# Scores and values' products of the first two batches as whole float32 products, with the order planned anew

## The chip, the cores and the metric

The kernel runs on one core of one Trainium2 chip. A core has five engines that run side by side and wait for each other by semaphores: TensorE (PE; its weight loads, PEld, stand as an engine of their own), VectorE (DVE), ScalarE (ACT), GpSimd (POOL) and SyncE (SP), which here only issues DMA transfers. The metric is the device time of one execution in microseconds (us), the median of several runs.

## The reference

Three stages follow each other, all in float32, with B=4 batches, 448 positions, 12 heads of 64:

```
scores = q @ k.T / 8 (causal mask); attn = softmax(scores); x = attn @ v      # per batch and head
u  = x + (relu(x.T @ w_tok1) @ w_tok2).T                                     # token mixing
y  = u + relu(u @ w_ch1) @ w_ch2                                             # channel mixing, 768 -> 1536 -> 768
h  = relu(y @ w_in); a, b = halves of h; n = layer norm of b
out = (a * (w_spatial @ n + b_spatial)) @ w_out                              # gated unit
```

q, k, v and w_spatial arrive as float32; the weights of token mixing, channel mixing and w_in, w_out arrive as 64-bit floats and are turned into float32 on the core.

## The kernel before

**Split operands.** Every product of two float32 operands is made of three: each operand is kept as two float32r parts, hi (ACT's cast) and lo (the difference, on POOL or DVE), and PE sums hi·hi, hi·lo and lo·hi (`mm3`, lines 227 to 229, and line 395). The product lo·lo is left out.

**Attention.** It runs over 24 pairs of heads (6 a batch). For pair n, `load` brings q, k (`stage`, first 896 columns) and v (512 columns). `split_qkv` makes `qh`, `ql` from q and k (ACT L343, POOL through L218) and hi and lo of v side by side in `vhl` (POOL, L215 and L218). `scores` issues 24 products (four chunks of queries, three terms, two heads; the heads lie on the two halves of the 64+64 rows), DVE adds the mask and takes the maximum (L403), ACT takes the exponential (L420), POOL normalizes (L437). `transposed` turns the weights over in five groups of 3 or 4 blocks (L478); of each group ACT takes hi (L481) and DVE lo (L218). `weighted` makes 8 products per head (L499 to L505) against `vhl`, so that the 128 output rows hold v's hi part and its lo part; ACT copies one half (L512) and DVE adds the other (L513).

**Token and channel mixing.** After every third pair a half batch goes through `token_mix`. `channel` takes a batch through 24 units: 12 of `ch1` (18 products 448 wide, L227 to L229, `ps<-uhl,whl`) and 12 of `ch2` (two tiles of 9, `ps<-hid,whl`, added to U on DVE, L676). The weights of a unit (`whl`, four buffers that take turns) are converted once: 72 pieces, each with three steps on DVE (L242, L244, L246), one on ACT and one on POOL, through the buffers `conv1`, `conv2` and `conv3`. Units 0 to 3 and 10 to 23 are converted into their `whl` buffer and stored to memory as well, units 4 to 9 come back by a load. `conv2` and `conv3` share their space with U of batches 2 and 3: so the values of pair 12, the first of batch 2, can only be written once the last piece that goes through `conv2` is done.

**The gated unit** comes last. Its weights (`wgv`, 22 pieces, `wf`) are converted into space that attention has left.

**What sets the order.** The kernel first records jobs (engine, planner's cost, keys read and written, priority, earliest start). `Plan.order` places them one by one, and each engine's instructions are issued in that order. Attention goes ahead of channel mixing by priority; pairs below `EAGER` may start at once, later ones at `START + (n - EAGER) * STEP` of the planner's own time.

Of the kernel before, what the change touches and what calls it, by code (L numbers as in the profile page):

```python
# [34 lines left out]

DIRECT = (*range(4), *range(10, 24))

EAGER, START, STEP = 12, 120.0, 28.0


class Buf:
# [128 lines left out]

@with_exitstack
def mixer_kernel(ctx: ExitStack, tc: tile.TileContext, qkv, wtok, wch, wgv, wsp, bsp, out):

# [16 lines left out]
    def buf(tag, shape, dtype, name):  # L192
        return plan.buf(tag, lambda t: sb.tile([128, *shape], dtype, tag=t, name=name))
# [10 lines left out]
    def act(n, psum=True):  # L204
        return (n * 0.833 + (55 if psum else 95)) / 1e3

    def dve(n, psum=True):
        return (n * 1.05 + 60) / 1e3 if psum else (n * 1.09 + 40) / 1e3

    def pool(n, two=True):  # L210
        return (n * 2.35 + 60) / 1e3 if two else (n * 0.83 + 230) / 1e3


    def hi_pool(hi, x):
        nc.gpsimd.tensor_scalar(hi, x, 1.0, 1.0, op0=ALU.mult, op1=ALU.mult)  # L215

    def lo_part(e, lo, x, hi):
        e.tensor_tensor(lo, x, hi.bitcast(F32), op=ALU.subtract)  # L218
# [104 lines left out]
    def load(n):  # L323
        st = stage[n % 2]
        operands[n] = {"st": st}
        p = n - 2.0
        src = qkv[n // NP, n % NP]
        job("SP", 0.07, lambda: nc.sync.dma_start(st.t[:, : 2 * S], src[:, : 2 * S]), w=[(st, "qk")], prio=p, size=458752)
        job("SP", 0.07, lambda: nc.sync.dma_start(st.t[:, 2 * S :], src[:, 2 * S :]), w=[(st, "v")], prio=p + 0.1, size=262144)

    def nominal(n):
        return 0.0 if n < EAGER else START + (n - EAGER) * STEP

    def split_qkv(n):
        st = operands[n]["st"]
        h = buf(f"qh{n % 2}", [2 * S], F32R, "qh")
        l = buf(f"ql{n % 2}", [2 * S], F32R, "ql")
        v = buf(f"v{n % 2}", [8, 128], F32R, "vhl")
        operands[n].update(h=h, l=l, v=v)
        p, at = n - 1.0, max(0.0, nominal(n) - 12)  # L340
        halves = [slice(0, S), slice(S, 2 * S)] if n == 0 else [slice(0, 2 * S)]
        for c in halves:
            job("ACT", act(c.stop - c.start, False), lambda c=c: nc.scalar.copy(h.t[:, c], st.t[:, c]), r=[(st, "qk")], w=[(h, c.start)], prio=p, at=at)  # L343
        for c in halves:
            if n == 0:
                job("DVE", dve(S, False), lambda c=c: lo_part(nc.vector, l.t[:, c], st.t[:, c], h.t[:, c]), r=[(st, "qk"), (h, c.start)], w=[(l, c.start)], prio=p)
            else:
                job("POOL", pool(2 * S), lambda c=c: lo_part(nc.gpsimd, l.t[:, c], st.t[:, c], h.t[:, c]), r=[(st, "qk"), (h, c.start)], w=[(l, c.start)], prio=p, at=at)

        def vs():  # L350
            return st.t[:, 2 * S :].rearrange("p (c d) -> p c d", d=64)

        job("POOL", pool(512, False), lambda: hi_pool(v.t[:, :, 0:64], vs()), r=[(st, "v")], w=[(v, "h")], prio=p + 0.6, at=at)
        job("POOL", pool(512), lambda: lo_part(nc.gpsimd, v.t[:, :, 64:128], vs(), v.t[:, :, 0:64]), r=[(st, "v"), (v, "h")], w=[(v, "l")], prio=p + 0.6, at=at)


    PLACE = {3: (0, 0), 0: (0, S), 2: (1, 0), 1: (1, 320)}
# [1 line left out]
    def scores(n):  # L359

        o = operands[n]
        h, l = o["h"], o["l"]
        big = buf(f"P{n % 2}", [1536], F32, "P32")
        o["big"] = big
        banks = [[bank([2 * j + k], "pss") for k in range(2)] for j in range(2)]
        s = stats[n % 2]
        split_keys = [(x, c) for x in (h, l) for c in ((0, S) if n == 0 else (0,))]

        def P(i):
            if i == 3:  # L370
                return big.t[:, : 2 * S].rearrange("p (j w) -> p j w", j=2)
            if i == 2:
                return big.t[:, 2 * S :].rearrange("p (j w) -> p j w", j=2)
            t = small[n % 2].t
            return (t[:, 0:384] if i == 1 else t[:, 384:512]).rearrange("p (j w) -> p j w", j=2)

        def pk(i, j):
            return (big, i, j) if i > 1 else (small[n % 2], i, j)

        o["P"], o["pk"] = P, pk  # L380

        def ps(i, j):
            k, o_ = PLACE[i]
            M, W = CHUNKS[i][1] - CHUNKS[i][0], CHUNKS[i][1]
            return banks[j][k].t[:M, o_ : o_ + W]

        def mms():
            for i in (3, 2, 1, 0):
                q0, q1 = CHUNKS[i]
                W = q1  # L390
                ks = [slice(2 * S - W, 2 * S), slice(S, S + W)]
                for k, (a, c) in enumerate(((h, h), (h, l), (l, h))):
                    for j in range(2):
                        r = slice(64 * j, 64 * j + 64)
                        nc.tensor.matmul(ps(i, j), a.t[r, q0:q1], c.t[r, ks[j]], start=(k == 0), stop=(k == 2))  # L395

        pkeys = [(banks[j][k], 0) for j in range(2) for k in range(2)]
        job("PE", 1.95, mms, r=split_keys, w=pkeys, touch=[big], prio=n, at=nominal(n))
        for i in (3, 2, 1, 0):
            M, W = CHUNKS[i][1] - CHUNKS[i][0], CHUNKS[i][1]  # L400
            for j in range(2):
                def ttr(i=i, j=j, M=M, W=W):
                    nc.vector.tensor_tensor_reduce(  # L403
                        out=P(i)[:M, j, :],
                        in0=ps(i, j),
                        in1=mask[:M, S - 128 : S - 128 + W] if j == 0 or M == 64 else mask[:M, S - W : S],
                        scale=-1.0 / 8.0,
                        scalar=3.0e38,
                        op0=ALU.add,
                        op1=ALU.min,  # L410
                        accum_out=s.t[:M, 0, 2 * i + j : 2 * i + j + 1],
                    )
# [12 lines left out]
        both = [(s, "sum", i, j) for i in range(4) for j in range(2)]

        def rcp():
            nc.vector.tensor_scalar_add(s.t[:, 2, :], s.t[:, 1, :], 1e-9)
            nc.vector.reciprocal(s.t[:, 2, :], s.t[:, 2, :])  # L429

        job("DVE", 0.15, rcp, r=both, w=[(s, "rs")], prio=n)
        for i in (3, 2, 1, 0):
            M, W = CHUNKS[i][1] - CHUNKS[i][0], CHUNKS[i][1]
            for j in range(2):
                def norm(i=i, j=j, M=M):
                    c = 2 * i + j
# [51 lines left out]
    def weighted(n, j):  # L488
# [22 lines left out]

        job("ACT", 0.55, lambda: nc.scalar.copy(x(), ps.t[64 - 64 * j : 128 - 64 * j, :S]), r=[(ps, 0)], w=[(u, hp, j)], prio=n)  # L512
        job("DVE", dve(S), lambda: nc.vector.tensor_tensor(x(), ps.t[r, :S], x(), op=ALU.add), r=[(ps, 0), (u, hp, j)], w=[(u, hp, j)], prio=n)  # L513


    wt = [buf(f"t{i}", [1536], F32R, f"wt{i}") for i in range(3)]
# [170 lines left out]
                ch2(b, u[1], u[2], i)  # L687


    for n in range(2):  # L690
        load(n)
    split_qkv(0)
    tok_keys = load_tok()
    for i in range(24):
        convert_channel(i)
    for b in range(B):
        U[b] = buf(f"U{b}", [KM, S], F32, f"U{b}")
    for n in range(NPAIR):
        if n:
            split_qkv(n)  # L700
        if n + 2 < NPAIR:
            load(n + 2)
        scores(n)
        for w, j in (("0", 0), ("a", 0), ("b", 0)):
            transposed(n, w, j)
        weighted(n, 0)
        for w in "ab":
            transposed(n, w, 1)
        weighted(n, 1)
        if n % 3 == 2:  # L710
            for s in ("x0", "x1", "x2", "x3", "h0", "h1", "u0", "u1", "u2"):
                token_mix(n // 3, s)
# [327 lines left out]
```

## Time and profile before

| | |
|---|---|
| median of 3 runs | 877.94 us (875.63 to 878.38) |
| profiled execution | 879.76 us, its span 878.0 us |
| granted TensorE clock, mean | 0.975 |
| PE busy | 817.4 us (93%), 4492 products |
| DVE, ACT, POOL busy | 502.9 us (57%), 358.3 us (41%), 345.2 us (39%) |
| DMA | 135.28 MB, mean 154 GB/s |

The busy shares are averages over unlike stretches, so they are read by stretch. Until about 272 us attention, the conversions and the first batch's channel mixing share all engines; until about 475 us PE works on the rest of attention and on channel mixing; then it goes on with channel mixing and the gated unit alone. PE's products overlap, so its busy time is larger than what they cost in a row: the distance between two starts is the price.

### The profile page before, as it was taken

The numbers are of one execution on the slowest core, as the hardware profiler recorded it, in microseconds if no ns is written. First come the engines' busy times: TensorE is split into PE (matmuls) and PEld (weight loads), VectorE is DVE, ScalarE is ACT, GpSimd is POOL, SyncE is SP. The second block draws the span as 40 slices with busy tenths as digits, with TensorE's granted clock in tenths as the row PEclk, the third lists the DMA queues.
The fourth block names the chain that finished last, engine by engine and source line by source line (L and its number), as shares of the span: only waits on it lengthen the run. The fifth ranks groups of instructions, "written<-read, shape, count | busy, mean of one in ns | idle before, by whom it ended". The sixth has DMA issues, their size and how long they took to land.

```text
span 878.0 us, 12877 instructions
## 1 busy us (share of the span) xinstructions
PE 817.4 (93%) x4492; PEld 730.0 (83%) x4492; DVE 502.9 (57%) x1300; ACT 358.3 (41%) x941; POOL 345.2 (39%) x465
## 2 busy tenths in 40 slices
PE   4678889999877999999999998999999999998998
PEld 4567778888766899999999887999998888877997
DVE  6989758898887575656465775312230242275441
ACT  6787857654235565444434223010032232232110
POOL 7978865747563453333334434100051340222000
PEclk9888889999989999999999999999999999999999
DMA  6545514897895243434268798566630000001112
GB/s 233 172 150 186 187 34 121 270 349 251 287 330 209 66 130 136 153 119 165 89 205 266 245 335 271 193 213 216 215 109 1 1 1 1 1 1 50 56 53 94
DMA packets 44273, 135.28 MB, mean 154 GB/s; under 512 B 4656, under 2 KB 12976, under 8 KB 44208
## 3 DMA queue, kind: packets, MB, share of 16 engines
q1 hardware_dynamic: 44208, 134.47, 45.5%
q8 instruction: 35, 0.57, 0.3%
q14 instruction: 30, 0.25, 0.1%
HBM read 110.07 MB, written 24.38 MB: 153 GB/s over the span
## 4 chain that ended last, share of the span: by engine, by line
PE 66%; DVE 19%; DMA 5%; ACT 4%; issue 3%; POOL 2%; SPq 0%; DVEq 0%; POOLq 0%; ACTq 0%
PE ps L227 9%; PE ps L229 9%; PE ps L228 9%; DMA dbl<-in_wgv 4%; PE pss L395 4%; PE pst L478 3%; DVE psw L242 3%; DVE psw L244 3%; DVE P L403 3%; PE pso L227 2%; PE psg L228 2%; PE psg L227 2%; PE psg L229 2%; PE pso L229 2%; PE pso L228 2%
## 5 line engine op out<-in xcount | busy, mean ns | idle before, releaser
L437 POOL TENSOR_SCALAR P<-P,stats 128x448 f32<-128x448 f32 (+1 forms) x192 | 87.4, 477 | 98.7 <-DVE stats L429 91.4
L227 PE MATMUL ps<-hid,whl 128*128 128x448 f32 x288 | 110.1, 382 | 12.1 <-DVE U L676 6.5
L227 PE MATMUL ps<-uhl,whl 128*128 128x448 f32 x288 | 109.5, 380 | 1.1 <-DVE hid L221 0.6
L218 POOL TENSOR_TENSOR uhl<-U,uhl 128x448 fp32r<-128x448 f32 x48 | 54.4, 1162 | 141.9 <-ACT uhl L643 116.8
L229 PE MATMUL ps<-hid,whl 128*128 128x448 f32 x288 | 107.7, 374 | 0.1
L228 PE MATMUL ps<-hid,whl 128*128 128x448 f32 x288 | 107.3, 372 | 0.0
L420 ACT ACTIVATE P<-P,stats 128x448 f32<-128x448 f32 (+1 forms) x192 | 96.1, 505 | 24.4 <-DVE stats L403 24.1
L229 PE MATMUL ps<-uhl,whl 128*128 128x448 f32 x288 | 105.5, 366 | 0.0
L228 PE MATMUL ps<-uhl,whl 128*128 128x448 f32 x288 | 105.4, 366 | 0.0
L676 DVE TENSOR_TENSOR U<-ps,U 128x448 f32<-128x448 f32 x96 | 59.6, 621 | 58.8 <-PE ps L229 58.5
L478 PE MATMUL pst<-ident,P 128*128 128x128 f32 x384 | 63.7, 294 | 21.6 <-POOL P L437 6.8
L403 DVE CUSTOM_DVE_ANT_0 P<-pss,mask 128x448 f32<-128x448 f32 (+1 forms) x192 | 70.2, 417 | 14.5 <-PE pss L395 11.7
L478 PEld LDWEIGHTS pst<-ident,P 128*128 128x128 f32 x384 | 46.4, 149 | 33.9 <-POOL P L437 10.3
L227 PEld LDWEIGHTS ps<-hid,whl 128*128 128x128 f32 x288 | 55.3, 192 | 20.9 <-ACT whl L294 8.2
L221 DVE SCALAR_TENSOR_TENSOR hid<-ps,hid 128x448 fp32r<-128x448 f32 x48 | 29.8, 622 | 57.3 <-ACT hid L660 57.3
L660 ACT ACTIVATE hid<-ps 128x448 fp32r<-128x448 f32 x48 | 26.0, 542 | 86.1 <-PE ps L229 85.8
L229 PEld LDWEIGHTS ps<-hid,whl 128*128 128x128 f32 x288 | 55.3, 192 | 5.8 <-POOL whl L218 0.8
L227 PEld LDWEIGHTS ps<-uhl,whl 128*128 128x128 f32 x288 | 54.2, 188 | 6.4 <-DVE hid L221 0.9
L228 PEld LDWEIGHTS ps<-hid,whl 128*128 128x128 f32 x288 | 55.3, 192 | 4.5
L218 DVE TENSOR_TENSOR Tab<-pst,Tab 128x384 fp32r<-128x384 f32 x96 | 51.3, 550 | 12.7 <-ACT Tab L481 12.3
L229 PEld LDWEIGHTS ps<-uhl,whl 128*128 128x128 f32 x288 | 54.1, 188 | 4.8 <-POOL whl L218 0.2
L481 ACT CAST Tab<-pst 128x384 fp32r<-128x384 f32 x96 | 44.7, 479 | 32.4 <-PE pst L478 31.0
(155 smaller groups left out, 1914.5 us busy)
## 6 DMA issues: line engine op xcount, KB each, us to landing
whl<-unit SPq DMA_DIRECT2D x78, 768.0 KB, 4.3
conv<-in_wch SPq DMA_DIRECT2D x72, 256.0 KB, 3.4
unit<-whl SPq DMA_DIRECT2D x18, 768.0 KB, 4.6
stage<-in_qkv SPq DMA_DIRECT2D x24, 448.0 KB, 3.5
stage<-in_qkv SPq DMA_DIRECT2D x24, 256.0 KB, 3.6
dbl<-in_wgv SPq DMA_DIRECT2D x16, 384.0 KB, 4.0
out_t<-gate SPq DMA_DIRECT2D x24, 224.0 KB, 1.9
unit<-conv SPq DMA_DIRECT2D x18, 256.0 KB, 3.8
```

What stands on the lines that cost most here:

```text
L218: e.tensor_tensor(lo, x, hi.bitcast(F32), op=ALU.subtract)
L221: nc.vector.scalar_tensor_tensor(lo, x, 0.0, hi.bitcast(F32), op0=ALU.max, op1=ALU.subtract)
L227: nc.tensor.matmul(ps, ah, bh, start=(first and i == 0), stop=False)
L228: nc.tensor.matmul(ps, ah, bl, start=False, stop=False)
L229: nc.tensor.matmul(ps, al, bh, start=False, stop=(last and i == n - 1))
L395: nc.tensor.matmul(ps(i, j), a.t[r, q0:q1], c.t[r, ks[j]], start=(k == 0), stop=(k == 2))
L403: nc.vector.tensor_tensor_reduce(out=P(i)[:M, j, :], in0=ps(i, j), in1=mask[:M, S - 128 : S - 128 + W] if j == 0 or M == 64 else mask[:M, ...
L420: nc.scalar.activation(P(i)[:M, j, :], P(i)[:M, j, :], AF.Exp, bias=s.t[:M, 0, c : c + 1], scale=-1.0, accum_out=s.t[:M, 1, c : c + 1])
L437: nc.gpsimd.tensor_scalar(P(i)[:M, j, :], P(i)[:M, j, :], s.t[:M, 2, c : c + 1], 1.0, op0=ALU.mult, op1=ALU.mult)
L478: nc.tensor.transpose(ps.t[:, c : c + M], src, ident[:M, :M])
L481: job("ACT", act(N), lambda: nc.scalar.copy(hl(0), ps.t[:, :N]), r=[(ps, 0)], w=[(b, part)], prio=n)
L676: job("DVE", dve(S), lambda d=d, ps=ps: nc.vector.tensor_tensor(u.t[:, d, :], ps.t[:, :S], u.t[:, d, :], op=ALU.add), r=[(ps, 0), *u_keys( ...
```

## The change

For batches 0 and 1 (pairs 0 to 11) the scores are issued as float32 products of q and k as they arrived (8 for a pair, not 24), with no split. The values are float32 products too: v is loaded into a tile of its own and not split; the transposes go in four groups of four blocks, each left by one copy (two on ACT, two on DVE); one product covers the first 128 columns for both heads, and six more write head 0 to output rows 0 to 63 and head 1 to rows 64 to 127, so that one ACT copy takes both heads to U. Pairs 12 to 23 keep their way. The planner has `EAGER, START, STEP` of 10, 100, 25 in place of 12, 120, 28, and its order is made anew.

```
-EAGER, START, STEP = 12, 120.0, 28.0
+WHOLE_S, WHOLE_V = (0, 1), (0, 1)
+EAGER, START, STEP = 10, 100.0, 25.0
...
+        if n // NP in WHOLE_V:
+            v = buf(f"v{n % 2}", [8, D], F32, "v")
+            operands[n]["v"] = v
+            job("SP", 0.07, lambda: nc.sync.dma_start(v.t, src[:, 2 * S :].rearrange("p (c d) -> p c d", d=D)), w=[(v, "h")], prio=p + 0.1, size=262144)
...
+        whole = n // NP in WHOLE_S
+        if whole:
+            st = o["st"]
+            split_keys, terms = [(st, "qk")], ((st, st),)
+        else:
+            h, l = o["h"], o["l"]
+            split_keys, terms = [(h, 0), (l, 0)], ((h, h), (h, l), (l, h))
+        last = len(terms) - 1
...
-                for k, (a, c) in enumerate(((h, h), (h, l), (l, h))):
+                for k, (a, c) in enumerate(terms):
...
+    def transposed_whole(n):
...
+        for g in range(4):
...
+            if g in (0, 2):
+                job("DVE", dve(N), lambda g=g, ps=ps, N=N: nc.vector.tensor_copy(t.t[:, 512 * g - 512 : 512 * g] if g else t0.t, ps.t[:, :N]), r=[(ps, 0)], w=[(b, g)], prio=n)
+            else:
+                job("ACT", act(N), lambda g=g, ps=ps, N=N: nc.scalar.copy(t.t[:, 512 * g - 512 : 512 * g], ps.t[:, :N]), r=[(ps, 0)], w=[(b, g)], prio=n)
...
+    def weighted_whole(n):
...
+            nc.tensor.matmul(ps.t[:, :S], v.t[:, 0:2, :].rearrange("p c d -> p (c d)"), t0.t, start=True, stop=False, skip_group_check=True)
+            for c, o, w in ((0, 64, 384), (1, 192, 256), (2, 320, 128)):
+                for j in range(2):
+                    r = slice(64 * j, 64 * j + 64)
+                    m = 768 * j + (0, 384, 640)[c]
+                    nc.tensor.matmul(ps.t[r, o:S], v.t[:, 2 + 3 * j + c, :], t.t[:, m : m + w], start=False, stop=(c == 2), skip_group_check=True)
...
+        job("ACT", act(S), lambda: nc.scalar.copy(u.t[:, hp, :], ps.t[:, :S]), r=[(ps, 0)], w=u_keys(n // NP, hp), prio=n)
```

On PE before, the end of the scores of pair 2 and both heads' values of pair 0 (`pss` scores, `pso` values, `T`, `Tab` the turned weights' hi and lo):

```order
L395 MATMUL pss<-qh 64x64 x2
L395 MATMUL pss<-ql,qh 64x64 x2
L395 MATMUL pss<-qh,ql 64x64 x2
L499 MATMUL pso<-T_298,vhl 128x448 x2
L501 MATMUL pso<-Tab,vhl 128x384 x2
L503 MATMUL pso<-Tab,vhl 128x256 x2
L505 MATMUL pso<-Tab,vhl 128x128 x2
L499 MATMUL pso<-T_298,vhl 128x448 x2
L501 MATMUL pso<-Tab,vhl 128x384 x2
L503 MATMUL pso<-Tab,vhl 128x256 x2
L505 MATMUL pso<-Tab,vhl 128x128 x2
```

Now, at the same place, the whole scores of pair 2 and the values of pair 0:

```order
L408 MATMUL pss<-stage_107 128x448 x2
L408 MATMUL pss<-stage_107 128x320 x2
L408 MATMUL pss<-stage_107 128x192 x2
L408 MATMUL pss<-stage_107 64x64 x2
L572 MATMUL pso<-T_254,v 128x448
L577 MATMUL pso<-PT,v 64x384 x2
L577 MATMUL pso<-PT,v 64x256 x2
L577 MATMUL pso<-PT,v 64x128 x2
```

The 24 products of a pair's scores have become 8, and the 16 of its values 7, with 64 output rows in six of them.

On DVE before, the end of the conversions (the steps from `conv` to `psw` and back to `conv`; `U<-pso` is pair 12's values, `U<-ps` channel mixing):

```order
L676 TENSOR_TENSOR U_378<-ps_3181,U_378 128x448
L242 TENSOR_SCALAR psw<-conv_117 128x256
L513 TENSOR_TENSOR U_3209<-pso,U_3209 64x448 x2
L676 TENSOR_TENSOR U_378<-ps_3198,U_378 128x448
L244 SCALAR_TENSOR_TENSOR psw<-conv_117,psw 128x256
L246 SCALAR_TENSOR_TENSOR conv_117<-conv_117,psw 128x256
L218 TENSOR_TENSOR T_3236<-pst,T_3236 128x448
L218 TENSOR_TENSOR Tab<-pst,Tab 128x384 x4
L403 ISA P_3309,stats_66<-pss,mask 128x448
```

Now, at the end of the conversions on DVE:

```order
L743 TENSOR_TENSOR U_312<-ps_2677,U_312 128x448
L245 TENSOR_SCALAR psw<-conv_119 128x256
L247 SCALAR_TENSOR_TENSOR psw<-conv_119,psw 128x256
L249 SCALAR_TENSOR_TENSOR conv_119<-conv_119,psw 128x256
L526 TENSOR_TENSOR U_2721<-pso,U_2721 64x448 x2
L743 TENSOR_TENSOR U_312<-ps_2710,U_312 128x448
L221 TENSOR_TENSOR T_2738<-pst,T_2738 128x448
L221 TENSOR_TENSOR Tab<-pst,Tab 128x384
L743 TENSOR_TENSOR U_312<-ps_2740,U_312 128x448
```

The place is nearly the same: pair 12's values follow the last piece or lie beside it, the scores of pairs 0 to 14 stand ahead of it in both orders, and those of pair 15 behind it. Behind the last `conv` row stand 607 rows of DVE before and 609 now.

## Rows read from the trace of the kernel before

**Rows 1.** Stretches: us, busy us (count) PE PEld DVE ACT POOL, clock, DMA, GB/s.

```profile
0.00:100.00 100.00, 73.51 (x498) 63.00 (x499) 84.58 (x276) 76.65 (x222) 83.05 (x124) 0.88 0.60 193
125.00:200.00 75.00, 73.29 (x470) 65.30 (x470) 65.01 (x189) 48.03 (x134) 44.05 (x62) 1.00 0.66 222
195.00:272.00 77.00, 67.01 (x327) 57.51 (x327) 66.00 (x164) 28.32 (x77) 44.15 (x61) 0.96 0.84 284
0.00:272.00 272.00, 228.05 (x1367) 197.38 (x1368) 225.31 (x665) 167.18 (x471) 184.76 (x266) 0.92 0.65 216
272.00:475.00 203.00, 198.45 (x1253) 182.47 (x1253) 118.67 (x322) 102.26 (x279) 80.38 (x112) 1.00 0.43 143
```

**Rows 2.** Waits from 195 to 272 us: total us, times, longest.

```profile
ACT whl L294 <- DVE conv L246: 46.0, 36, 2.2
```

**Rows 3.** DVE timeline, the last conversion step: start us, us, engine, line, operation.

```profile
271.09 0.42 DVE L246 SCALAR_TENSOR_TENSOR conv<-conv,psw 128x256 uint32<-128x256 uint32 x1
```

**Rows 4.** DVE groups, 0 to 272 us: count, busy us, mean ns, idle.

```profile
L218 DVE TENSOR_TENSOR Tab<-pst,Tab 128x384 fp32r<-128x384 f32 x52 | 27.7, 550 | 3.2 <-ACT Tab L481 2.9
...
L513 DVE TENSOR_TENSOR U<-pso,U 64x448 f32<-64x448 f32 x26 | 16.1, 620 | 3.3 <-ACT U L512 3.0
...
L676 DVE TENSOR_TENSOR U<-ps,U 128x448 f32<-128x448 f32 x22 | 13.6, 617 | 1.1 <-PE ps L229 1.0
...
L218 DVE TENSOR_TENSOR T<-pst,T 128x448 fp32r<-128x448 f32 x13 | 8.1, 620 | 1.7 <-ACT T L481 1.5
L221 DVE SCALAR_TENSOR_TENSOR hid<-ps,hid 128x448 fp32r<-128x448 f32 x12 | 7.4, 620 | 4.2 <-ACT hid L660 4.2
```

**Rows 5.** DVE copy from PSUM (L943): count, ns min/median/max, first and last start.

```profile
L943 DVE COPY gate<-pso x12: 623/624/625, 803.0 to 874.3; 128x448 f32<-128x448 f32 x12
```

**Rows 6.** ACT groups from 0 to 272 us.

```profile
L481 ACT CAST Tab<-pst 128x384 fp32r<-128x384 f32 x52 | 24.2, 478 | 4.7 <-PE pst L478 3.7
...
L343 ACT CAST qh<-stage 128x896 fp32r<-128x896 f32 x16 | 15.1, 941 | 8.9 <-POOL P L437 3.3 <-PE pss L395 2.2 <-DMA stage<-in_qkv 2.1
L512 ACT COPY U<-pso 64x448 f32<-64x448 f32 x26 | 13.7, 527 | 4.9 <-PE pso L505 3.2 <-POOL whl L218 0.8 <-issue 0.2
...
L481 ACT CAST T<-pst 128x448 fp32r<-128x448 f32 x14 | 7.4, 530 | 1.7 <-PE pst L478 1.6
```

**Rows 7.** POOL groups from 0 to 272 us.

```profile
L218 POOL TENSOR_TENSOR ql<-stage,qh 128x896 fp32r<-128x896 f32 x16 | 33.7, 2104 | 6.1 <-ACT qh L343 5.9
L218 POOL TENSOR_TENSOR vhl<-stage,vhl 128x512 fp32r<-128x512 f32 x15 | 19.5, 1299 | 1.2
...
L215 POOL TENSOR_SCALAR vhl<-stage 128x512 fp32r<-128x512 f32 x15 | 9.5, 631 | 7.5 <-PE pso L505 4.9 <-DMA stage<-in_qkv 2.6
```

**Rows 8.** PE timeline around one pair's scores and one head's values.

```profile
396.20 0.36 PE L228 MATMUL ps<-hid,whl 128*128 128x448 f32 x1
396.40 0.37 PE L229 MATMUL ps<-hid,whl 128*128 128x448 f32 x1
396.69 0.47 PE L395 MATMUL pss<-qh 64*128 64x448 f32 x2
397.01 0.37 PE L395 MATMUL pss<-ql,qh 64*128 64x448 f32 x2
...
398.41 0.67 PE L499 MATMUL pso<-T,vhl 128*128 128x448 f32 x2
...
399.67 0.41 PE L227 MATMUL ps<-hid,whl 128*128 128x448 f32 x1
```

**Rows 9.** Chain of waits, a run of seven float32 transposes.

```profile
350.99 0.77 PE pst L478 x7
```

**Rows 10.** The gated unit's conversions, and its first products.

```profile
L246 DVE SCALAR_TENSOR_TENSOR wf<-dbl,psw x22: 501/553/689, 460.6 to 555.3; 128x384 uint32<-128x384 uint32 x16, 128x512 uint32<-128x512 uint32 x6
...
L227 PE MATMUL psg<-uhl,whl x96: 361/365/370, 658.7 to 757.6; 128*128 128x448 f32 x96
```

**Rows 11.** The page's DMA issues: count, KB each, us to landing.

```profile
stage<-in_qkv SPq DMA_DIRECT2D x24, 448.0 KB, 3.5
```

More of the change, by code (lines that the diff above doesn't have):

```diff
@@ L328, in load, with split_qk @@
         job("SP", 0.07, lambda: nc.sync.dma_start(st.t[:, : 2 * S], src[:, : 2 * S]), w=[(st, "qk")], prio=p, size=458752)
-        job("SP", 0.07, lambda: nc.sync.dma_start(st.t[:, 2 * S :], src[:, 2 * S :]), w=[(st, "v")], prio=p + 0.1, size=262144)
+        if n // NP in WHOLE_V:
[3 more added lines that the diff above has]
+        else:
+            job("SP", 0.07, lambda: nc.sync.dma_start(st.t[:, 2 * S :], src[:, 2 * S :]), w=[(st, "v")], prio=p + 0.1, size=262144)
     def nominal(n):
         return 0.0 if n < EAGER else START + (n - EAGER) * STEP
-    def split_qkv(n):
+    def split_qk(n):
         st = operands[n]["st"]
@@ L337, in split_qkv, with split_v @@
         l = buf(f"ql{n % 2}", [2 * S], F32R, "ql")
-        v = buf(f"v{n % 2}", [8, 128], F32R, "vhl")
[L339 to L348, printed above, removed]
+        operands[n].update(h=h, l=l)
+        p, at = n - 1.0, max(0.0, nominal(n) - 12)
+        job("ACT", act(2 * S, False), lambda: nc.scalar.copy(h.t, st.t[:, : 2 * S]), r=[(st, "qk")], w=[(h, 0)], prio=p, at=at)
+        job("POOL", pool(2 * S), lambda: lo_part(nc.gpsimd, l.t, st.t[:, : 2 * S], h.t), r=[(st, "qk"), (h, 0)], w=[(l, 0)], prio=p, at=at)
+    def split_v(n):
+        st = operands[n]["st"]
+        v = buf(f"v{n % 2}", [8, 128], F32R, "vhl")
+        operands[n]["v"] = v
+        p, at = n - 0.4, max(0.0, nominal(n) - 12)
         def vs():
-            return st.t[:, 2 * S :].rearrange("p (c d) -> p c d", d=64)
-        job("POOL", pool(512, False), lambda: hi_pool(v.t[:, :, 0:64], vs()), r=[(st, "v")], w=[(v, "h")], prio=p + 0.6, at=at)
-        job("POOL", pool(512), lambda: lo_part(nc.gpsimd, v.t[:, :, 64:128], vs(), v.t[:, :, 0:64]), r=[(st, "v"), (v, "h")], w=[(v, "l")], prio=p + 0.6, at=at)
+            return st.t[:, 2 * S :].rearrange("p (c d) -> p c d", d=D)
+        job("POOL", pool(512, False), lambda: hi_pool(v.t[:, :, 0:64], vs()), r=[(st, "v")], w=[(v, "h")], prio=p, at=at)
+        job("POOL", pool(512), lambda: lo_part(nc.gpsimd, v.t[:, :, 64:128], vs(), v.t[:, :, 0:64]), r=[(st, "v"), (v, "h")], w=[(v, "l")], prio=p, at=at)
     PLACE = {3: (0, 0), 0: (0, S), 2: (1, 0), 1: (1, 320)}
@@ L361, in scores @@
         o = operands[n]
-        h, l = o["h"], o["l"]
+        whole = n // NP in WHOLE_S
[6 more added lines that the diff above has]
+        last = len(terms) - 1
         big = buf(f"P{n % 2}", [1536], F32, "P32")
@@ L366, in scores @@
         s = stats[n % 2]
-        split_keys = [(x, c) for x in (h, l) for c in ((0, S) if n == 0 else (0,))]
         def P(i):
@@ L391, in mms @@
                 ks = [slice(2 * S - W, 2 * S), slice(S, S + W)]
-                for k, (a, c) in enumerate(((h, h), (h, l), (l, h))):
+                for k, (a, c) in enumerate(terms):
                     for j in range(2):
                         r = slice(64 * j, 64 * j + 64)
-                        nc.tensor.matmul(ps(i, j), a.t[r, q0:q1], c.t[r, ks[j]], start=(k == 0), stop=(k == 2))
+                        nc.tensor.matmul(ps(i, j), a.t[r, q0:q1], c.t[r, ks[j]], start=(k == 0), stop=(k == last))
         pkeys = [(banks[j][k], 0) for j in range(2) for k in range(2)]
-        job("PE", 1.95, mms, r=split_keys, w=pkeys, touch=[big], prio=n, at=nominal(n))
+        job("PE", 2.5 if whole else 1.95, mms, r=split_keys, w=pkeys, touch=[big], prio=n, at=nominal(n))
         for i in (3, 2, 1, 0):
@@ L513, in weighted, with P, block, mms @@
         job("DVE", dve(S), lambda: nc.vector.tensor_tensor(x(), ps.t[r, :S], x(), op=ALU.add), r=[(ps, 0), (u, hp, j)], w=[(u, hp, j)], prio=n)
+    def transposed_whole(n):
+        o = operands[n]
+        def P(i):
+            return o["P"](i).rearrange("p j w -> p (j w)")
+        def block(j, i, c):
+            W, (k0, k1) = CHUNKS[i][1], CHUNKS[c]
+            return P(i)[:, slice(W + k0, W + k1) if j else slice(W - k1, W - k0)]
+        later = [(j, i, c) for j in range(2) for c, i in ((1, 1), (1, 2), (1, 3), (2, 2), (2, 3), (3, 3))]
+        t0 = buf(f"T0{n % 2}", [S], F32, "T0")
+        t = buf(f"A{n % 2}", [12 * 128], F32, "PT")
+        for g in range(4):
+            ps = bank(early if n < NP else banks_tm, "pst")
+            b = t if g else t0
+            N = 512 if g else S
+            keys = [o["pk"](i, j) for i in range(4) for j in range(2)] if g == 0 else [o["pk"](i, j) for j, i, c in later[4 * g - 4 : 4 * g]]
+            def mms(g=g, ps=ps):
+                if g == 0:
+                    blocks = [(q0, P(i)[:, q1 - 64 : q1 + 64]) for i, (q0, q1) in enumerate(CHUNKS)]
+                else:
+                    blocks = [(128 * k, block(*x)) for k, x in enumerate(later[4 * g - 4 : 4 * g])]
+                for c, src in blocks:
+                    nc.tensor.transpose(ps.t[:, c : c + 128], src, ident)
+            job("PE", 0.44, mms, r=keys, w=[(ps, 0)], touch=[b], prio=n)
+            if g in (0, 2):
+                job("DVE", dve(N), lambda g=g, ps=ps, N=N: nc.vector.tensor_copy(t.t[:, 512 * g - 512 : 512 * g] if g else t0.t, ps.t[:, :N]), r=[(ps, 0)], w=[(b, g)], prio=n)
+            else:
+                job("ACT", act(N), lambda g=g, ps=ps, N=N: nc.scalar.copy(t.t[:, 512 * g - 512 : 512 * g], ps.t[:, :N]), r=[(ps, 0)], w=[(b, g)], prio=n)
+        PT[n] = t0, t
@@ new lines, in weighted_whole, with mms @@
+    def weighted_whole(n):
+        v = operands[n]["v"]
+        ps = bank(early if n < NP else banks_tm, "pso")
+        t0, t = PT[n]
+        u = U[n // NP]
+        hp = n % NP
+        def mms():
+            nc.tensor.matmul(ps.t[:, :S], v.t[:, 0:2, :].rearrange("p c d -> p (c d)"), t0.t, start=True, stop=False, skip_group_check=True)
[4 more added lines that the diff above has]
+                    nc.tensor.matmul(ps.t[r, o:S], v.t[:, 2 + 3 * j + c, :], t.t[:, m : m + w], start=False, stop=(c == 2), skip_group_check=True)
+        job("PE", 2.8, mms, r=[(v, "h"), (t0, 0), *((t, g) for g in (1, 2, 3))], w=[(ps, 0)], prio=n)
+        job("ACT", act(S), lambda: nc.scalar.copy(u.t[:, hp, :], ps.t[:, :S]), r=[(ps, 0)], w=u_keys(n // NP, hp), prio=n)
@@ L687, in channel, with split @@
                 ch2(b, u[1], u[2], i)
+    def split(n):
+        if n // NP not in WHOLE_S:
+            split_qk(n)
+        if n // NP not in WHOLE_V:
+            split_v(n)
     for n in range(2):
         load(n)
-    split_qkv(0)
     tok_keys = load_tok()
@@ L698, in mixer_kernel @@
     for n in range(NPAIR):
-        if n:
-            split_qkv(n)
+        split(n)
+        scores(n)
         if n + 2 < NPAIR:
             load(n + 2)
[L703 to L709, printed above, removed]
+        if n // NP in WHOLE_V:
+            transposed_whole(n)
+            weighted_whole(n)
+        else:
+            for w, j in (("0", 0), ("a", 0), ("b", 0)):
+                transposed(n, w, j)
+            weighted(n, 0)
+            for w in "ab":
+                transposed(n, w, 1)
+            weighted(n, 1)
         if n % 3 == 2:
```

## The prediction, made before the changed kernel was run

> **What bounds the kernel now.** I read the stretches first, then the waits, then the groups. The stretches [rows 1] split the run at 272 us. From 272 to 475 us PE is busy 198.5 of 203 us at full clock and every other engine has slack: that part, and what follows, is PE's own work. Before 272 us no engine is full: DVE is busy 225.3 us, PE 228.1, POOL 184.8, ACT 167.2. What ends at 272 us is the conversion of the channel weights: its last DVE step starts at 271.09 and takes 0.42 us [rows 3]. Pair 12's values wait for it, by the shared space of conv2, and pair 15's scores follow it. From 195 us on DVE is 66 of 77 us busy; ACT waits 46.0 us of them for conversion steps [rows 1, 2]. In the first 100 us DVE, POOL and ACT are busy 84.6, 83.1 and 76.7 us, and PE's clock is 0.88: there each pair goes round a ring of all four engines, and none is full. So what the change can win is the date of the last conversion, 271.5 us; the 606.5 us behind it hold the same work, for the rows on DVE behind that point are 609 against 607, with scores up to pair 14 ahead in both.
>
> **What DVE, ACT and POOL lose.** Before 272 us DVE spends 27.7 + 8.1 us on lo parts of turned weights and 16.1 us on adding heads [rows 4], together 51.9. Twelve of the 13 pairs lose that. In its place come two copies a pair, of 448 and 512 columns: 0.62 us [rows 5] and 0.62 x 512/448 = 0.71, so 12 x 1.33 = 16.0 us. Pair 12 keeps one T and four Tab, 2.8 us (its additions now follow the last conversion). So DVE does 51.9 - 16.0 - 2.8 = 33 us less, 192 in place of 225. ACT loses per pair 0.94 (qh) + 4 x 0.48 + 0.53 (turned weights) + 2 x 0.53 (heads) = 4.4 and gains two copies of 512 columns and one of 448, each near 0.53 x 512/448 = 0.61 [rows 6], 1.7 in all: 2.7 less. POOL loses 2.10 + 1.30 + 0.63 = 4.0 a pair [rows 7]. Neither of the two is the last to end after 195 us, so their relief counts only in the first 100 us, where it shortens the ring.
>
> **What PE gains and loses.** No row shows a whole float32 product that isn't a transpose; I bound it. At full clock a 448-wide product follows another after 0.20 us (396.20 to 396.40), and a pair's scores take 396.69 to 398.41 = 1.72 us for three terms with both heads side by side: the second row "x2" starts 0.32 us and not 0.40 after the first [rows 8]. The nearest float32 row is the transposes: seven of 128 columns in 0.77 us, 0.11 us each [rows 9], 1.9 times what a 128-column share of a 0.20 us product would take (0.057). Low end for the scores: one term, 0.57 us, times 1.9 = 1.1 us. For the value I take the arithmetic of the split: a whole product holds the three terms and lo·lo besides, so four terms, 4/3 x 1.72 = 2.3 us. High end: four terms and the heads one behind the other, 4.6 us. Values: one head takes 398.41 to 399.67 = 1.26 us, a pair 2.5. The old eight products already are all four partial products, hi and lo of v side by side. Now the first 448 columns serve both heads at once, and 384 + 256 + 128 = 768 columns go per head. With four passes at 0.20/448 us a column this is 4 x (448 + 768) columns = 2.2 us if the heads' column halves run side by side as their row halves do, and 3.6 if not; with 1.9 passes 1.0. Entering a new shape costs 0.1 us (396.40 to 396.69 in place of 0.20), twice as the scores begin (0.32 in place of 0.20 behind it); I add 0.3 for the two changes of shape, for 2.5, and another 0.3 for halves that don't start together: 2.8. The transposes stay at 16 a pair. Per pair: +0.6 +0.3 = +0.9, with ends at -2.1 (1.1 + 1.0 against 4.2) and +4.3 (4.6 + 3.9 against 4.2). Times 12: +11 us, between -25 and +52.
>
> No row here shows how many passes a float32 product takes. The Trainium skill, page "FP8 and Floating Point Precision", section TensorE Precision Notes, has a true FP32 product as four passes through the array. By it the change buys the relief of three engines with work on the fullest one: the sum would be the same 2.3 us for scores, and the transposes' low end would fall away.
>
> **The sum.** PE's work ahead of 272 us, at full clock: 15 scores x 1.72 = 26; 13 x 16 transposes x 0.11 = 23; 26 heads x 1.26 = 33; channel mixing, 12 first halves of 18 products and 22 tiles of 9 (L221 and L676) [rows 4], 414 x 0.203 = 84; three half batches of token mixing, each 12 transposes, 22 products of 384 and 18 of 448 columns, 8.8: 26. Together 192, so 80 of the 272 us are lost. Now it is 192 + 11, and the new order has some 5 us of the fourth half batch's token mixing ahead of the last conversion: 208. In the first stage the ring is shorter by 2.8 us of DVE, 2.7 of ACT and 4.0 of POOL a pair, but a pair asks of PE 2.3 + 1.8 + 2.8 = 6.9 us. I choose 85 us for the stage up to the ninth pair's scores, with 65 us of PE's work in it (nine scores 21, seven pairs' transposes and values 32, token mixing 12): 76% against the 73.5 of 100 us that PE was busy before [rows 1]. The other 143 us go at the share between 98% (125 to 200 us) and 87% (195 to 272 us), 92% [rows 1], and with the clock and order not quite as planned 90%: 158 us. The last conversion then ends at 85 + 158 = 243. Against that stands DVE: 192 us of work at the share of before (225/272 = 83%) needs 231, with the 47 idle us of before 239. So both engines allow 243, and PE is the later. Span: 878 - (271.5 - 243) - 5 = 844.5; the profiled execution was 1.8 us over its span, 879.76, and that is 1.8 us over the median of the runs: 846 for the profile, 844.5 as a median. I say 846, as nothing is put down for stalls in the new order.
>
> **What hides the rest.** The load of q and k for pair n+2 now waits for the scores of pair n and not for its split, a few us later; the other stage buffer covers it for one pair, over 8 us, against a transfer that lands in 3.5 us [rows 11]. If that cover goes, PE waits some 4 us in single places. On SP these loads stand among conversion loads, and a load of whl for units 4 to 9 stands in one run behind pair 10's v, which waits for pair 8's values: conversions behind it wait with it. The gated unit's conversions end at 555 us and their first use is at 658.7 [rows 10]: 100 us of cover, of which an earlier attention takes nothing.
>
> **Rivals.** (1) The forecast: 0.60, 832 to 860. (2) Float32 products overlap badly, the heads partly one behind the other, +2.5 us a pair in place of +0.9: 12 x 1.6 = 19, so 865. For it: nothing before shows column halves at all. Against: row halves do overlap [rows 8]. 0.18. (3) Slower: the heads don't overlap at all on either kind of halves, +4.3 a pair: 12 x 3.4 = 41 more than forecast, of which a fuller PE gives back some 4: 883. It decides from +3.7 a pair, where (880 - 846)/12 = 2.8 is added to 0.9. 0.07. (4) Cheaper products, as the transposes are: PE's part falls by up to 36 us, but DVE's 231 us then bind, 12 earlier than 243: 834, and less if DVE gets fuller, 826. 0.10. (5) The relief isn't on the path: units 10 to 23 are converted into one of four whl buffers, free only when PE is done with the unit four before; then the date is PE's and the plan's, and the time stays at 876 to 881. Against it ACT's 46.0 us of waiting for DVE's steps [rows 2]. 0.05.
>
> **Chances.** Faster by over 0.3% (2.6 us, about the spread of the runs): 0.60 + 0.18 + 0.10 = 0.88. Within: 0.04 of the fifth. Slower: 0.07 + 0.01 = 0.08. The range 826 to 869 holds the first, second and fourth but for their tails; the third and fifth, 0.12, and some 0.07 of tails lie outside.
>
> The Trainium skill, page "TensorEngine Tiling (Array Packing)", section Key Properties, says that different tiles of the array load and multiply in parallel; by that column halves overlap as row halves do, which makes the third rival unlikely. No run here shows it for column halves.
>
> **What would show it.** In the new profile: scores of a pair at full clock near 2.3 us and values near 2.8; the last conversion step near 243 us; DVE busy about 192 us ahead of it; PE busy over 95% from there to the gated unit, as before. Scores over 3.5 us or values over 3.5 us would be the second or third rival; a last conversion at 265 us with DVE idle over 60 us would be the fifth. The forecast is wrong in kind if the conversion ends early and the time behind it grows past 606 us.

## The result and the profile after

| | before | after |
|---|---|---|
| median | 877.28 us (4 runs, 875.63 to 878.38) | 844.15 us (4 runs, 843.37 to 848.05) |
| ratio, 95% interval | | 0.9633 (0.9599 to 0.9667) |
| span of the profiled execution | 878.0 us | 841.8 us |
| end of the last conversion step | 271.5 us | 244.0 us |
| span behind it | 606.5 us | 597.8 us |

The forecast was 846 us and the range 826 to 869; the measured time is 844.15 us, 3.7% shorter than before. The page of the changed kernel, busy us by engine and the granted clock in 40 slices:

```profile
PE 801.4 (95%) x4372; PEld 699.1 (83%) x4372; DVE 472.8 (56%) x1238; ACT 325.9 (39%) x880; POOL 298.1 (35%) x430
...
PEclk9999999999999999999999999999999999999999
```

The stretches of the changed kernel, in the columns of [rows 1]:

```profile
0.00:100.00 100.00, 78.08 (x476) 51.50 (x477) 85.84 (x297) 67.42 (x217) 61.47 (x121) 1.00 0.73 236
0.00:244.00 244.00, 213.65 (x1246) 165.70 (x1246) 194.80 (x603) 134.37 (x409) 135.86 (x230) 0.99 0.72 233
245.00:475.00 230.00, 229.14 (x1408) 211.66 (x1409) 134.53 (x350) 109.57 (x293) 88.56 (x119) 0.99 0.50 170
```

Up to the last conversion DVE is busy 194.8 us where it was 225.3, ACT 134.4 (167.2), POOL 135.9 (184.8). PE's granted clock there is 0.99 (0.92), in the first 100 us 1.00 (0.88). Behind it PE is full, as before. Ahead of it no engine is full all the way: in the first 100 us DVE is the busiest, and from 100 to 143 us PE is full by itself:

```profile
100.00:143.00 43.00, 42.59 (x224) 37.33 (x223) 22.77 (x47) 11.45 (x25) 6.38 (x8) 1.00 0.68 221
```

The DVE timeline with the last conversion step, which answers to [rows 3]:

```profile
243.60 0.42 DVE L249 SCALAR_TENSOR_TENSOR conv<-conv,psw 128x256 uint32<-128x256 uint32 x1
```

The DVE groups up to 245 us, which answer to [rows 4]: the copies that came, and pair 12's lo parts that stayed:

```profile
L558 DVE COPY PT<-pst 128x512 f32<-128x512 f32 x12 | 8.2, 684 | 0.0
...
L558 DVE COPY T<-pst 128x448 f32<-128x448 f32 x12 | 7.4, 617 | 0.0
...
L221 DVE TENSOR_TENSOR Tab<-pst,Tab 128x384 fp32r<-128x384 f32 x4 | 2.2, 541 | 0.1
```

The PE timeline around one pair's whole scores, and then one pair's whole values (answers to [rows 8]):

```profile
154.63 0.37 PE L232 MATMUL ps<-uhl,whl 128*128 128x448 f32 x1
154.92 2.15 PE L408 MATMUL pss<-stage 64*128 64x448 f32 x16
157.00 0.47 PE L230 MATMUL ps<-uhl,whl 128*128 128x448 f32 x1
...
172.65 1.02 PE L572 MATMUL pso<-T,v 128*128 128x448 f32 x2
173.60 1.51 PE L577 MATMUL pso<-PT,v 128*64 128x384 f32 x12
175.05 0.47 PE L230 MATMUL ps<-hid,whl 128*128 128x448 f32 x1
```

From the start of the scores to the next operation pass 157.00 - 154.92 = 2.08 us (1.72 before), and for both heads' values 175.05 - 172.65 = 2.40 us (2 x 1.26). Other pairs at full clock show 2.08, and 2.29 to 2.40. Each whole product stands in the trace as two records: x16 for 8 products, x2 for one.

### The profile page after: what moved, and what is told of

Its sections match the earlier page's. It is cut to its first block, busy times and chain, and to the rows that moved or that the text cites. A ratio compares the mean times of both kernels' runs of the same rounds, so it can differ in the third digit from the quotient of the medians.

```text
span 841.8 us, 12478 instructions
## 1 busy us (share of the span) xinstructions
PE 801.4 (95%) x4372; PEld 699.1 (83%) x4372; DVE 472.8 (56%) x1238; ACT 325.9 (39%) x880; POOL 298.1 (35%) x430
## 4 chain that ended last, share of the span: by engine, by line
PE 79%; DVE 14%; DMA 3%; ACT 2%; issue 2%; POOL 0%; DVEq 0%; ACTq 0%
PE ps L230 13%; PE ps L232 13%; PE ps L231 13%; PE pss L408 4%; DVE P L416 3%; PE pst L491 3%; PE pso L230 2%; PE pso L231 2%; PE pso L232 2%; PE psg L231 2%; PE psg L232 2%; PE psg L230 2%; PE psv L230 2%; PE psv L231 2%; PE psv L232 2%; DVE psw L247 2%
## 5 line engine op out<-in xcount | busy, mean ns | idle before, releaser
L230 PE MATMUL ps<-hid,whl 128*128 128x448 f32 x288 | 108.2, 376 | 4.6 <-DVE U L743 4.5
L232 PE MATMUL ps<-hid,whl 128*128 128x448 f32 x288 | 106.0, 368 | 0.0
L231 PE MATMUL ps<-hid,whl 128*128 128x448 f32 x288 | 105.8, 367 | 0.0
L230 PEld LDWEIGHTS ps<-hid,whl 128*128 128x128 f32 x288 | 54.3, 189 | 10.6 <-DVE U L743 4.8
L230 PEld LDWEIGHTS ps<-uhl,whl 128*128 128x128 f32 x288 | 54.1, 188 | 6.1 <-DMA whl<-unit 1.0
L232 PEld LDWEIGHTS ps<-hid,whl 128*128 128x128 f32 x288 | 54.4, 189 | 4.7
L232 PEld LDWEIGHTS ps<-uhl,whl 128*128 128x128 f32 x288 | 54.1, 188 | 4.6
L231 PEld LDWEIGHTS ps<-hid,whl 128*128 128x128 f32 x288 | 54.5, 189 | 4.1
L231 PEld LDWEIGHTS ps<-uhl,whl 128*128 128x128 f32 x288 | 54.3, 188 | 3.7
L221 POOL TENSOR_TENSOR whl<-conv,whl 128x256 fp32r<-128x256 f32 x54 | 38.2, 731 | 51.0 <-ACT whl L297 51.0
L906 DVE BATCH_NORM_STATS2 bias<-v 128x6 f32<-128x512 f32 x14 | 9.7, 695 | 72.3 <-ACT v L903 72.3
L554 PE MATMUL pst<-ident,P 128*128 128x128 f32 x192 | 28.4, 282 | 11.3 <-POOL P L450 5.3
```

The costliest lines, as they stand in the source:

```text
L230: nc.tensor.matmul(ps, ah, bh, start=(first and i == 0), stop=False)
L231: nc.tensor.matmul(ps, ah, bl, start=False, stop=False)
L232: nc.tensor.matmul(ps, al, bh, start=False, stop=(last and i == n - 1))
L554: nc.tensor.transpose(ps.t[:, c : c + 128], src, ident)
```

## The experiments

All twelve are variants of the changed kernel, but for the first, which is one of the kernel before. The table sums them up; "date" is the end of the last conversion step, "behind" the span less the date, busy us are up to the date, the clock too. Dates, busy us and clocks are of one profiled execution each. e5, e6, e7, e8 and e11 keep the changed kernel's order on every engine; the others have theirs planned anew.

| run | median us | ratio to before (95%) | date | behind | DVE | ACT | POOL | PE | clock |
|---|---|---|---|---|---|---|---|---|---|
| before | 877 | | 271.5 | 606.5 | 225 | 167 | 185 | 228 | 0.92 |
| changed | 844.15 | 0.963 (0.960-0.967) | 244.0 | 598 | 195 | 134 | 136 | 214 | 0.99 |
| e1 | 881.42 | 1.006 (1.004-1.008) | 275.7 | 604 | 224 | 166 | 184 | 227 | 0.92 |
| e2 | 850.04 | 0.970 (0.968-0.972) | 244.5 | 600 | 195 | 135 | 138 | 210 | 0.99 |
| e3 | 881.54 | 1.006 (1.003-1.009) | 275.1 | 602 | 223 | 157 | 161 | 227 | 0.96 |
| e4 | 862.27 | 0.985 (0.981-0.988) | 261.3 | 600 | 196 | 146 | 163 | 218 | 0.95 |
| e5 | 876.33 | 1.000 (0.997-1.003) | 278.8 | 597 | 226 | 135 | 136 | 230 | 0.93 |
| e6 | 867.76 | 0.990 (0.984-0.995) | 270.0 | 596 | 196 | 161 | 136 | 227 | 0.91 |
| e7 | 860.35 | 0.979 (0.972-0.987) | 260.0 | 600 | 197 | 134 | 176 | 221 | 0.94 |
| e8 | 854.43 | 0.974 (0.967-0.980) | 255.1 | 597 | 195 | 135 | 136 | 232 | 0.98 |
| e9 | 889.99 | 1.016 (1.012-1.020) | 289.0 | 597 | 234 | 136 | 137 | 234 | 0.92 |
| e10 | 839.90 | 0.960 (0.956-0.964) | 244.6 | 593 | 194 | 134 | 128 | 217 | 0.99 |
| e11 | 843.10 | 0.962 (0.958-0.966) | 245.0 | 596 | 195 | 135 | 136 | 221 | 0.98 |
| e12 | 839.58 | 0.958 (0.955-0.962) | 237.3 | 600 | 191 | 127 | 119 | 215 | 0.98 |

**e1, the plan's constants alone.** The kernel before with

```
-EAGER, START, STEP = 12, 120.0, 28.0
+EAGER, START, STEP = 10, 100.0, 25.0
```

> The kernel before with EAGER, START, STEP of 10, 100, 25 and no whole product. Theory A (the gain is the earlier last conversion, bought by what DVE, ACT and POOL no longer do): the engines' work is that of before, so 870 to 884 us, the last conversion step at 262 to 278 us. Theory B (the gain is the new plan's constants): half of the gain or more is here, 860 us or less.

881.42 us: nothing is won, 0.6% is lost. Theory B falls.

**e2, the whole products with the old constants.** The same two lines the other way round, in the changed kernel.

> The changed kernel with EAGER, START, STEP of 12, 120, 28 as before. Theory A: within 1% of the changed kernel, 838 to 853 us. Theory B: 860 us or more.

850.04 us, as theory A has it. The date is that of the changed kernel; against it the new constants are worth 3 us of span, nearly all behind that date (845.0 against 841.8), and 6 us by the medians.

**e3, whole scores alone; e4, whole values alone.**

```
-WHOLE_S, WHOLE_V = (0, 1), (0, 1)
+WHOLE_S, WHOLE_V = (0, 1), ()        # e3; in e4 (), (0, 1)
```

> Whole scores for batches 0 and 1, values split as before; new constants. DVE loses nothing but 1.6 us, ACT 0.94 and POOL 2.1 us a pair, PE gains 0.36 us a pair (2.08 against 1.72, from the changed kernel's trace). Theory A with DVE as the engine that counts: 865 to 880 us. Theory C (the shorter ring of the first 100 us and PE's higher clock count, whichever engine is relieved): about half of the gain, 855 to 864 us.

> Whole values for batches 0 and 1, scores split as before; new constants. DVE loses 2.6 us, ACT 1.8 and POOL 1.9 us a pair, PE 0.15 (2.35 against 2.5). Theory A with DVE as the engine that counts: nearly the whole gain, 843 to 855 us. Theory C: about half of it, 856 to 865 us.

Whole scores alone gain nothing against the same constants without them (881.54 against 881.42), though ACT and POOL have 9 and 23 us less to do. The stretches up to the date of e3, and then of e4:

```profile
0.00:275.00 275.00, 226.53 (x1263) 187.41 (x1263) 222.53 (x662) 156.57 (x457) 161.43 (x255) 0.96 0.65 214
```

```profile
0.00:261.00 261.00, 217.54 (x1344) 176.36 (x1344) 195.98 (x605) 145.57 (x423) 163.02 (x243) 0.95 0.67 224
```

In e3 DVE is as busy as before the change and the date doesn't move: it isn't ACT or POOL that binds there, and DVE is the engine that kept its load. In e4 DVE has its 196 us and the date comes 14 us earlier than in e1, which is only half of the way to 244. So theory A, with DVE as the only engine that counts, holds for e3 and is too simple for e4: once DVE is relieved, what ACT and POOL still do for the split scores seems to keep the date back (e6 and e7 put such load back by itself). The two halves of the change are worth 0 and 19 us alone, and 37 together.

**e5, DVE's load put back.** The two copies are made three times; the order stays.

```
-lambda g=g, ps=ps, N=N: nc.vector.tensor_copy(...)
+lambda g=g, ps=ps, N=N: [nc.vector.tensor_copy(...) for _ in range(3)]
```

> The changed kernel, but each of DVE's two copies of turned weights per pair is made three times: 2 x (0.62 + 0.68) = 2.6 us of DVE a pair, 31 us in all, what the change took from DVE; order as planned for the changed kernel. Theory A (DVE's load sets the date of the last conversion): that date back at 262 to 275 us, 862 to 878 us. Theory P (PE is the later engine since the change, as the prediction had it): DVE's idle time takes most of it, 844 to 855 us.

876.33 us: the whole gain is gone. The copies and the stretch of e5:

```profile
L558 DVE COPY PT<-pst x36: 680/691/693, 19.5 to 232.6; 128x512 f32<-128x512 f32 x36
L558 DVE COPY T<-pst x36: 614/624/625, 21.5 to 230.6; 128x448 f32<-128x448 f32 x36
```

```profile
0.00:279.00 279.00, 229.77 (x1241) 177.21 (x1242) 225.73 (x651) 135.29 (x410) 136.06 (x230) 0.93 0.63 204
```

48 more copies of 0.66 us, 31.6 us, move the date by 34.8: 1.1 us for each us of DVE. PE has the very products of the changed kernel, and yet its clock falls from 0.99 to 0.93.

**e6, ACT's load put back; e7, POOL's; e8, more for PE.** In e6 ACT's two copies are made three times. In e7

```
+                    if whole and i == 0 and j == 1:
+                        for _ in range(2):
+                            nc.gpsimd.tensor_tensor(spare.t, big.t[:, 448:1344], big.t[:, 448:1344], op=ALU.subtract)
```

and in e8

```
-                for k, (a, c) in enumerate(terms):
+                for k, (a, c) in enumerate(terms * (2 if whole else 1)):
...
-                        nc.tensor.matmul(..., start=(k == 0), stop=(k == last))
+                        nc.tensor.matmul(..., start=(whole or k == 0), stop=(whole or k == last))
```

> The changed kernel, but each of ACT's two copies of turned weights per pair is made three times: 4 x 0.6 = 2.4 us of ACT a pair, 29 us in all, about what the change took from ACT. Theory A: ACT has slack, 844 to 852 us. Theory C (the pair's way round all engines counts in the first 100 us): the nine pairs there are each 2 us later, 858 to 870 us.

> The changed kernel with two more POOL operations of 128x896 (2.1 us each, into space that is free) behind a pair's normalization: 4.2 us a pair, 50 us in all, what the change took from POOL. Theory A: POOL has slack, 844 to 852 us. Theory C: POOL is again as full as before in the first 100 us, 855 to 870 us.

> The changed kernel with every whole score product of batches 0 and 1 issued twice: 2.08 us more PE work a pair, 25 us in all, nothing else changed. Theory P: PE is the later engine, 864 to 872 us. Theory A: PE has slack ahead of the last conversion, 846 to 858 us.

(`spare` is the space that `ql` has in the pairs with split scores.) The stretches up to the date of e6, e7 and e8, and one pair's doubled scores in e8:

```profile
0.00:270.00 270.00, 226.79 (x1240) 173.31 (x1241) 196.22 (x603) 160.66 (x457) 135.98 (x230) 0.91 0.64 210
```

```profile
0.00:260.00 260.00, 220.59 (x1240) 171.06 (x1241) 196.53 (x603) 134.43 (x409) 175.77 (x254) 0.94 0.66 218
```

```profile
0.00:255.00 255.00, 232.35 (x1432) 182.29 (x1433) 195.12 (x603) 134.59 (x409) 136.18 (x230) 0.98 0.69 223
```

```profile
161.91 3.88 PE L408 MATMUL pss<-stage 64*128 64x448 f32 x32
165.72 0.47 PE L230 MATMUL ps<-uhl,whl 128*128 128x448 f32 x1
```

The doubled scores cost 165.72 - 161.91 = 3.81 us a pair, 1.73 and not 2.08 more, so 21 us in all and not the 25 expected; POOL's added operations came to 40 us and not 50. ACT's 26 us move the date by 26, POOL's 40 by 16, PE's 21 by 11. ACT's slack, which theory A gave it, isn't there: theory C holds for e6 and e7. Theory P falls with e8: only half of PE's added work shows in the date. With these prices e4 comes out near: against the changed kernel it has 11 us more ACT and 27 us more POOL, and 4.3 less PE (12 x 0.36), which at 1.0, 0.4 and 0.5 a us is 11 + 11 - 2 = 20 us; its date is 17 later. But they can't be added up where DVE has its load: e3 has 28 us more DVE, 22 more ACT and 26 more POOL than the changed kernel, which would make 31 + 22 + 10 = 63 us, and its date is 31 later, what DVE's part gives by itself. In e6 the values of a pair wait for the added copies; whether ACT's load or the pair's longer way makes the price, no run shows for ACT.

**e9, DVE's load put back where no pair waits for it.** Behind the second copy, four operations a pair:

```
...
+                        for _ in range(4):
+                            nc.vector.tensor_tensor(spare.t[:, :512], t.t[:, 512:1024], t.t[:, 512:1024], op=ALU.subtract)
```

> The changed kernel with 4 more DVE operations of 128x512 a pair behind DVE's second copy of turned weights, into space that is free: about 2.5 us of DVE a pair, some 30 us in all, as in the run that made the copies three times, but nothing of a pair waits for them. If DVE's load sets the date of the last conversion: 866 to 878 us, as that run (876). If what counts is that a pair's way round the engines gets longer: 848 to 860 us.

889.99 us, over both expectations. The added operations of e9, who waited for them, and its stretch:

```profile
L563 DVE TENSOR_TENSOR spare<-PT 128x512 f32<-128x512 f32 x48 | 36.9, 769 | 1.6
```

```profile
  POOL ql L221: 7.2, 2
```

```profile
0.00:289.00 289.00, 233.51 (x1248) 180.88 (x1248) 233.54 (x654) 136.09 (x411) 136.90 (x230) 0.92 0.62 201
```

48 x 0.77 = 36.9 us move the date by 45. A part of that is the experiment's own: the free space is that of `ql`, for which pairs 12 and 13 wait (7.2 us of POOL), and as the planner counts the added use of that space, the order behind the twelfth pair's scores isn't the changed kernel's. Up to these scores the order is the same; they start in the changed kernel, e5 and e9 at

```profile
182.16 2.15 PE L408 MATMUL pss<-stage 64*128 64x448 f32 x16
211.30 2.15 PE L408 MATMUL pss<-stage 64*128 64x448 f32 x16
219.25 2.15 PE L408 MATMUL pss<-stage 64*128 64x448 f32 x16
```

Up to there DVE is busy 142.5, 168.4 and 173.9 us: 26 us more put the scores 29 us back in e5, 31 more put them 37 back in e9, so 1.1 and 1.2 a us. So it is DVE's load in itself, and not the length of one pair's way, that sets the price. Why it is rather more than 1 isn't settled; the lower clock (0.92) goes with it.

**e11, the heads' column halves one after the other.**

```
-            for c, o, w in ((0, 64, 384), (1, 192, 256), (2, 320, 128)):
-                for j in range(2):
+            for j in range(2):
+                for c, o, w in ((0, 64, 384), (1, 192, 256), (2, 320, 128)):
```

> The changed kernel with the six products on column halves in another order: all three of head 0, then all three of head 1. If the halves overlap only when the two heads alternate, a pair's values go from 2.35 to about 3.6 us (768 columns x 4 x 0.45 ns = 1.4 us more), 15 us of PE in all, of which the run with more PE work gave 0.4 back in time: 848 to 854 us. If they don't overlap anyway: unchanged, 843 to 846 us.

843.10 us, as the second expectation has it, but for another reason. The PE timeline of e11 around one pair's values:

```profile
173.12 1.02 PE L572 MATMUL pso<-T,v 128*128 128x448 f32 x2
174.07 2.21 PE L577 MATMUL pso<-PT,v 128*64 128x384 f32 x12
176.22 0.47 PE L230 MATMUL ps<-hid,whl 128*128 128x448 f32 x1
```

The values take 176.22 - 173.12 = 3.10 us and not 2.40: the halves do overlap when the heads alternate. The 12 x 0.7 = 8 us of PE come out of its idle time ahead of the date, which is 1 us later (245.0).

**e10, whole values in all batches; e12, whole scores and values in all batches.** `WHOLE_V = (0, 1, 2, 3)`, and in e12 `WHOLE_S` too.

> Whole values in all four batches, whole scores in the first two as changed. Pairs 12 to 14 relieve DVE ahead of the last conversion by 3 x 2.6 us, and behind it, where PE is full, a pair costs PE 0.15 us less (2.35 against 2.5): 12 x 0.15 = 2 us. Theory A: 834 to 843 us, faster than the changed kernel. Rival: PE's price of the column halves is higher where PE is full: 845 us or more.

> Whole scores and whole values in all four batches. Behind the last conversion PE is full, and there a pair's scores cost 0.36 us more and its values 0.15 less: 12 x 0.21 = 2.5 us more than the changed kernel, less what three pairs ahead of the date relieve (up to 8 us): 838 to 847 us, and 3 to 5 us over the run with whole values alone in all batches. Rival (the relief of the other engines counts behind that date too): as fast as that run or faster.

839.90 and 839.58 us: both beat the kernel before, and stand 0.5% under the changed one, with intervals that touch its own (0.956 to 0.964 and 0.955 to 0.962 against 0.960 to 0.967), so that they are faster than it is likely but not shown. e10's date is the changed kernel's: the relief of DVE that I had expected ahead of it isn't there (194.2 us against 194.8). Its gain lies behind it (593 against 598), where PE is full. A pair's values cost 2.29 us there, split ones 2.38 (357.13 to 359.51 us in the changed kernel), which is some 1 us in all; and PE has 4 us more of its work done ahead of the date (217 against 214), by the new order. e12's date is 7 us earlier and its span behind it 7 us longer than e10's. I had expected e12 to be 3 to 5 us over e10; they are equal.

## Why the prediction was right, step by step

- **What bounds it.** Right. In the changed kernel and the twelve variants the span behind the date stays between 593 and 604 us, while the date goes from 237 to 289: the time is the date and some 598 us. The date was forecast at 243 and is 244.0.
- **The relief.** The sizes are right: DVE 33 us, measured 30.5 (copies of 0.617 and 0.684 us for 0.62 and 0.71); ACT 12 x 2.7 = 32, measured 33; POOL 12 x 4.0 = 48, measured 49. That ACT's and POOL's relief counts only in the first 100 us was too narrow, for ACT at least: e6 has the eighth pair's scores at 90 us (76 in the changed kernel), which is 14 of its 26 us, and the other 12 come later.
- **PE's price.** The term that was mis-sized. Four partial products were right, the heads' overlap was better than allowed for: scores 2.08 us (2.3 put down), values 2.29 to 2.40 (2.8), so +0.2 us a pair and 2 to 3 us in all, not +0.9 and 11. By the Trainium skill, page "FP8 and Floating Point Precision", section TensorE Precision Notes, a true FP32 product is four passes. The trace agrees: the whole product of 448 columns takes 0.95 us (172.65 to 173.60) with a change of shape at either end, 4.7 times the 0.20 us of a split term; within the scores a record of 448 columns starts at 155.40 and the next shape at 155.78, so two records take some 0.75 us, 3.7 times, and nowhere near the transposes' 1.9. The second and third rival fall by the rows of scores and values, the fourth by those of the scores.
- **PE is the later engine.** Wrong. e8 and e11 show PE with cover: 21 us more cost 11, 8 us cost 1. DVE comes first (e3, e5); ACT's and POOL's load count at once when they come back. I had set both engines' need side by side and chose PE; that both gave about 240 is why the date came out right, and as far as the choice of the engine goes that was luck. DVE's own sum, 192 us of work and 47 idle, came out at 194.8 and 49.2. PE's sum with the measured prices would give some 241 in place of 243, an estimate: 8.5 us less work, of which 5.5 lies in the first stage, whose 85 us stay. Nor is one engine the later one all the way: from 100 to 143 us PE is busy 42.6 of 43.
- **The clock.** The sum has it only in the 90% share of PE ("with the clock and order not quite as planned"). Up to the date it went from 0.92 to 0.99, so PE spent less time at the lower of its two levels (1.2 and 2.4 GHz). It goes with the other engines' load: with the same products it is 0.99 in the changed kernel, 0.93 in e5 and 0.91 in e6. But its price is small where the runs show it. The four runs of the changed kernel have mean clocks of 0.998, 0.996, 0.984 and 0.981 and times of 843.4, 843.8, 844.5 and 848.1 us; those of e6 go from 0.969 to 0.986 with 2.5 us between the slowest and the fastest. In e12 the clock of the first 100 us is 0.95, against 1.00 in the changed kernel with the same pairs, and the ninth pair's scores start at 83.3 us against 83.1.
- **The first stage.** Right: 85 us put down for the ninth pair's scores, which start at 83 us.
- **The cover.** Right for the gated unit: DVE's last conversion step for it starts at 536.9 us, its first product at 621.3. The prediction names a risk for the conversions, whose transfers stand behind waiting loads on SP, and puts nothing down for it; the chain of the changed kernel has a new wait, 10.9% of the stretch from 143 to 245 us, on transfers of `conv<-in_wch`, the second of those shown for the last piece. No run shows what it costs:

```profile
189.71 5.50 DMA conv<-in_wch
236.88 5.63 DMA conv<-in_wch
```

- **Behind the date** 5 us were expected to be done ahead; 8.7 were won. e2 shows 3 of them as the plan's.
- **The fifth rival** (the relief isn't on the path) fell: in e5 the date goes back with DVE's load alone, and the order is the same on every engine.

What stays open: how much of the 27.5 us is the clock and how much the engines' load, since no experiment was made to change the one without the other. The spread within one kernel, up to 5 us for 0.017 of the mean clock, where the kernels before and after differ by 0.021 (0.975 and 0.996, profiled), speaks for the smaller part being the clock's; that is an estimate.

## What to carry to other kernels

When a stage ends with one engine's queue and three others are nearly as busy, relieving the others alone gives nothing (e3), relieving the first gives half of what both give (e4), and the rest comes with the next ones; put an engine's load back in place, one at a time, to see which counts. A product that costs the fullest engine more can be cheaper if that engine idles in the stage in question. Price each term in the stage in which it lies: in e11 8 us on PE cost 1, in e8 21 us cost 11, while behind the date PE is busy 229 of 230 us.

## What the runs showed of the hardware

- A whole float32 product of 448 columns took 0.95 us with a change of shape before and behind it (from 172.65 to 173.60 us), some 0.75 us within the scores, and stands in the trace as two records, against 0.20 us for a float32r product; a float32 transpose of 128 columns took 0.11 us [rows 9].
- Whole float32 products overlap on the two halves of the rows (scores of two heads 2.08 us) and on the two halves of the columns (values 2.40 us with the heads in turn, 3.10 with one head after the other).
- PE's granted clock up to the date was 0.99, 0.93 and 0.91 for the same products on PE: in the changed kernel, with 31 us more on DVE, and with 26 us more on ACT.
